# Layer A's residual addition on GpSimd beside attention, and the last closing statistics queued later

## The chip, the cores and the metric

The program runs on one core of a Trainium2 chip. The metric is the device time of one execution in microseconds. Three runs of the kernel before gave 1640.73, 1641.19 and 1642.21 us.

## What is computed

Four layers, A B A B, each added to its input x (2048 rows of 640 columns, 32 heads of 20):

```
x = x + A(layernorm(x)); x = x + B(layernorm(x)); and both once more

A: q, k, v = split(x @ wqkv)            # linear attention, phi(t) = t+1 or exp(t), + 1e-6
   out = phi(q) (phi(k)^T v) / (phi(q) . sum(phi(k)) + 1e-6) @ wo

B: in 4 segments of 512 rows, per head:
   a_dot = softmax(q k^T * scale + mask) v          # within the segment
   a_mem = phi(q) M / (phi(q) z + 1e-6)             # M, z: memory of the earlier segments
   out = (g * a_mem + (1 - g) * a_dot) @ wo;  M += phi(k)^T v;  z += sum(phi(k))
```

The mask leaves, for key k and query q of a segment, what lies on one side of the diagonal. g is a sigmoid of beta.

## The kernel before

**Tiling.** The rows are cut in 4 segments of 4 tiles of 128 rows. Products are done with fp16 operands in an upper and a lower part (three matmuls for one), so nearly every evacuation of a bank has a ScalarE copy of the upper part and a VectorE subtraction for the lower. There are 8 PSUM banks (`bank`) and a pool of 11 row buffers, tag `row`, which hold x, its residual input `xo`, its new value `xn`, the normed `xh`, the transposed outputs `oT` and layer A's queries `pqi`.

**Layer A.** A first pass over all segments (`g_first`) makes one matrix of keys and rows and writes the queries' features to DRAM (`pqd`). Then `merge` folds the matrix with the weights of v and o into one weight `wm`. The second pass makes the outputs segment by segment: `a_head` and `p_read` load the queries of a tile (line 924, on SyncE's queue), multiply them by z (line 934), sum them per head (938), add and scale (939), take the reciprocal (940) and multiply by it on GpSimd (942); this is the reading. `turn` transposes the result. `a_second` then multiplies by `wm` in two halves of 320 columns, 15 matmuls each, and `o_half` scales each half and adds the residual: by one VectorE instruction (line 499), or, with `later`, by a ScalarE copy (496) and a GpSimd addition (497). It then stores the tile (line 988, a DMA issue on ScalarE's queue) and takes its mean and variance (`moments`, 368 to 373: statistics and aggregate on VectorE, a power on GpSimd), shifts the mean (378), norms the tile (`normed`, 404) and transposes it for layer B.

**Layer B.** `b_project` makes v, q and k of a segment from the transposed tiles; q and k are split (`split_store`, 1020 to 1035) and go through DRAM. `attention` works in groups of 4 heads, eight groups a segment, each in three stretches: scores, row maxima (1224), their split in two parts (1233, 1234), a transposition and a small ScalarE copy that brings them back as two rows (1242 to 1247), scores the other way round, exponentials (1263), a GpSimd select that cuts them at the diagonal (1270), the weighing by v (1286), and the division. `read_mem` adds the memory's part. `b_out` multiplies by wo and adds the residual; it is what is called closing rows in the text below. It always uses the later path, except at the very end, and stores on ScalarE's queue (1185) behind an instruction named `anchor`. In the first layer B it also takes the statistics of each new tile (`gather`, 386 and 387), one tile late, behind the lower part of the next transposition, and after the last tile `settle` makes the inverse deviations of all four (393 on VectorE, 394 on GpSimd). They are used when the rows are loaded again for the next layer A.

**What runs beside what.** `run` merges two streams, the dense layers and attention, by estimated costs of TensorE. The four segments of layer A's second pass are followed by the projection of the same segment in layer B; from the end of segment 0's projection on, attention of the earlier segments runs between them. The closing rows of segments 0 and 1 are woven into the projections of segments 2 and 3, and `a_head` of the next segment follows directly behind them in the projection of segment 2.

**What sets the order.** TensorE's instructions run in the order in which the program names them. On the other engines Tile's planner queues them at build time by priority, which is the order of naming, among those that its own model of time holds ready; `tc.high_priority(offset=n)` moves a block n places ahead, or behind where n is negative, and `tc.issue_after(i)` puts a block behind instruction i on i's engine. On the chip each engine works its queue off in that order, waits included. `a_second` uses `self.added`, the last VectorE addition of `o_half`, as such a fence: for the shift of the mean and for the lower parts of two transpositions. Its `moments` go 40 places behind.

Of the kernel before, what the change touches and what calls it, by code (L numbers as in the profile page):

```python
# [25 lines left out]
NT = SEG // P  # L26
# [118 lines left out]
class Kernel:  # L145
# [816 lines left out]
    def a_second(self, src, dst, s, L, box, norm):  # L962


        nc = self.nc
        o, oT = box["o"], box["oT"]
        xT = self.x_t() if norm else None
        xh = []
        for i in range(NT):
            if i + 3 < NT:  # L970
                yield from self.p_read(L, s, i + 3, o)
            x = self.load_x(src, s, i, "xo")
            xn = self.row("xn")
            t = iter(())
            if i + 1 < NT:
                oT.append(self.new_oT())
                t = self.turn(o[i + 1], oT[i + 1], 0)
            for n in range(2):
                yield from (c for c in [next(t, None)] if c)
                self.o_half(oT[i], L["wm"], "G", x, xn, n)  # L980
                if norm and i > 0 and n == 0:
                    with self.tc.issue_after(self.added.ins):
                        m = self.shift(*m)
                    if i != 2:
                        xh.append(self.normed(*m))
                yield self.COST_N
            r = s * SEG + i * P
            self.q_x.dma_start(dst[r:r + P], xn)
            if norm:
                if i > 1:  # L990
                    yield from self.turn(xh[i - 2], xT, i - 2, self.added)
                if i == 2:
                    with self.tc.issue_after(self.upper.ins):
                        xh.append(self.normed(*m))
                with self.tc.high_priority(offset=-40):
                    m = self.moments(xn, False)
        box["xT"] = xT

        def tail():
            t = self.turn(xh[NT - 2], xT, NT - 2)  # L1000
            yield next(t)
            cost = next(t)
            with self.tc.issue_after(self.lower.ins), self.tc.issue_after(self.spread.ins):
                xh.append(self.normed(*self.shift(*m)))
            yield cost
            yield from self.turn(xh[NT - 1], xT, NT - 1)
        box["tail"] = tail()
# [141 lines left out]
    def b_out(self, st, wo, src, dst, norm, after=None):  # L1149

        yield lambda: st.get("attended")
        nc, s = self.nc, st["s"]
        made = []
        mv = self.sb.tile([P, NT, 2], F32, tag="mv4", name="mv4", bufs=NSEG) if norm else None
        begun = [None, None]
        turned = lambda i: self.o_turned(st, i)
        t = iter(()) if "oT" in st else turned(0)
        oT = st["oT"]
        if st.get("ends"):
            ahead = turned(1)  # L1160
            yield from (c for c in [next(t, None)] if c)
            yield next(ahead)
            for n in range(2):
                begun[n] = self.proj_n(oT[0], wo, 0, n, cs=range(3))
                yield 9 * HN * COL
        yield from t
        for i in range(NT):
            x = self.load_x(src, s, i, "xo")
            xn = self.row("xn")
            if i + 1 < NT:  # L1170
                t = ahead if i == 0 and st.get("ends") else turned(i + 1)
            else:
                t = self.o_turned(after, 0) if after and after.get("attended") else iter(())
            for n in range(2):
                yield from (c for c in [next(t, None)] if c)
                self.o_half(oT[i], wo, "B", x, xn, n, later=not st.get("ends"), begun=begun[n] if i == 0 else None)
                split = st.get("ends") and i == NT - 1
                if split:
                    c = slice(n * HN, (n + 1) * HN)
                    self.q_x.dma_start(dst[s * SEG + i * P:s * SEG + i * P + P, c], xn[:, c])  # L1180
                yield self.COST_N
            r = s * SEG + i * P
            if not split:
                with nullcontext() if st.get("ends") else self.tc.issue_after(self.anchor.ins):
                    self.q_x.dma_start(dst[r:r + P], xn)
            made.append(xn)
            if norm and i > 0:
                with self.tc.issue_after(self.lower.ins):
                    self.gather(made[i - 1], mv[:, i - 1])
        if norm:  # L1190
            yield 0.0
            self.gather(made[-1], mv[:, NT - 1])
            st["norm"] = self.settle(mv, False)


    def stacks(self, st, g):
# [367 lines left out]
```

## Time and profile before

| | us |
|---|---|
| median of three runs | 1641.19 |
| the profiled execution | 1644.86 |
| its span, first to last instruction | 1641.3 |
| TensorE busy | 1607.0 |
| VectorE busy | 1223.1 |
| ScalarE busy | 1016.0 |
| GpSimd busy | 518.2 |

PE is TensorE's matmuls, PEld its weight loads, DVE VectorE, ACT ScalarE, POOL GpSimd, SP SyncE; a q behind the name is the engine's queue. L499 is line 499 of the kernel. `xn<-ps,ioG,xo` says what an instruction writes and reads. The TensorE clock was granted in full for 0.999 of the span.

### The profile page before, as it was taken

What the parts mean: (1) busy time and instruction counts of PE and PEld (TensorE: products, weight loads), DVE (VectorE), ACT (ScalarE), POOL (GpSimd) and SP (SyncE); (2) the same over time, 40 slices, a digit from 0 to 9 for tenths busy, and PEclk for the clock granted to TensorE, in tenths of its full rate; (3) what the DMA queues carried; (4) which work ended last, traced back from release to release, by engine and by line L of the source; (5) the groups of instructions that cost most, each with busy time, mean ns of one, the idle gap of its engine ahead of it and who ended that gap; (6) DMA issues with size and microseconds to landing.
All of it is one profiled execution on the core that took longest, in us unless ns stands there. A gap on an engine that the chain in (4) does not pass through costs nothing.

```text
span 1641.3 us, 37783 instructions
## 1 busy us (share of the span) xinstructions
PE 1607.0 (98%) x13772; PEld 1016.2 (62%) x13772; DVE 1223.1 (75%) x3953; ACT 1016.0 (62%) x1955; POOL 518.2 (32%) x1077
## 2 busy tenths in 40 slices
PE   9999999999999999999999999999999999999998
PEld 6777776654665575456567777756546546645555
DVE  8777794688877787768764557837888888878772
ACT  6877743367567657667666544433775675676773
POOL 3421132133234423433341301211333433333552
PEclk9999999999999999999999999999999999999999
DMA  6434734423222422352211303534232232323432
GB/s 227 161 140 153 275 125 160 141 70 112 95 71 88 137 100 94 109 191 70 66 46 47 107 33 125 177 131 131 68 112 90 102 111 88 118 84 108 152 101 97
DMA packets 110345, 189.30 MB, mean 115 GB/s; under 512 B 14160, under 2 KB 69840, under 8 KB 107728
## 3 DMA queue, kind: packets, MB, share of 16 engines
q1 hardware_dynamic: 97536, 141.02, 26.6%
q0 software_dynamic: 3264, 24.91, 4.2%
q10 hardware_dynamic: 9360, 20.98, 3.3%
q8 instruction: 108, 1.77, 0.5%
q14 instruction: 77, 0.63, 0.1%
HBM read 109.32 MB, written 77.00 MB: 114 GB/s over the span
## 4 chain that ended last, share of the span: by engine, by line
PE 73%; ACT 5%; DVE 3%; issue 1%; DMA 1%; POOL 0%; SPq 0%; ACTq 0%; DVEq 0%
PE ps L431 29%; PE ps L417 14%; PE ps L1286 9%; PE ps L1259 4%; PE ps L348 4%; PE ps L758 4%; PE ps L1218 4%; ACT pe L1263 3%; PE ps L473 2%; PE ps L1299 1%; PE ps L1065 1%; DVE ps L1224 1%; PE ps L1055 1%; DMA pqi<-pqd 1%; ACT xh L404 0%
## 5 line engine op out<-in xcount | busy, mean ns | idle before, releaser
L1224 DVE CUSTOM_DVE_ANT_0 ps<-ps,maskw 128x384 f32<-128x384 f32 (+3 forms) x1024 | 472.4, 519 | 47.2 <-PE ps L1218 43.5
L1263 ACT ACTIVATE pe<-ps,lsc 128x512 f32<-128x512 f32 x640 | 391.7, 696 | 84.3 <-PE ps L1259 69.8
L1270 POOL TENSOR_SCALAR_AFFINE_SELECT pe<-pe 128x256 f32<-128x256 f32 (+1 forms) x640 | 238.7, 382 | 342.9 <-ACT pe L1263 338.2
L431 PEld LDWEIGHTS <-xT 128*128 128x128 f16 x2760 | 267.8, 98 | 103.6 <-issue 5.3
L431 PEld LDWEIGHTS <-oT 128*128 128x128 f16 x1920 | 185.8, 98 | 77.2 <-issue 4.6
L1286 PE MATMUL ps<-pe,v 128*32 128x512 f32 (+3 forms) x2048 | 156.5, 436 | 7.6 <-DVE nat L1026 3.2
L417 PE MATMUL ps<-xT,w_Bq 128*128 128x512 f16 x600 | 142.2, 382 | 3.6 <-ACT pe L1263 2.9
L1224 DVE DVE_READ_ACCUMULATOR2_ANT mg<- 128x1 f32 x1024 | 143.4, 140 | 0.0
L431 PE MATMUL ps<-w_Bo,oT 128*128 128x320 f16 x960 | 140.6, 299 | 1.9 <-DVE tmp L1309 0.6
L417 PE MATMUL ps<-xT,w_Bk 128*128 128x512 f16 x600 | 141.6, 379 | 0.4 <-DVE tmp L1309 0.4
L431 PE MATMUL ps<-wm,oT 128*128 128x320 f16 x960 | 140.6, 299 | 0.5
L431 PE MATMUL ps<-w_Bv,xT 128*128 128x320 f16 x960 | 139.7, 299 | 0.3 <-ACT pe L1263 0.3
L758 PE MATMUL ps<-pk,xs 128*128 128x321 f16 (+1 forms) x960 | 137.0, 300 | 1.5 <-DVE v L778 0.6
L431 PE MATMUL ps<-w_Aq,xT 128*128 128x320 f16 x960 | 138.4, 299 | 0.0
L1259 PE MATMUL ps<-qs,ks 62*128 62x512 f16 (+3 forms) x1024 | 130.2, 299 | 3.5 <-ACT pe L1263 2.4
L1026 DVE SCALAR_TENSOR_TENSOR nat<-ps,nat 128x512 f16<-128x512 f32 x80 | 55.2, 690 | 94.0 <-ACT r L1025 70.6
L431 PE MATMUL ps<-w_Ak,xT 128*128 128x320 f16 x840 | 119.4, 299 | 0.0
L758 PEld LDWEIGHTS <-xs 128*128 128x128 f16 x960 | 93.0, 97 | 39.6 <-issue 2.7
L1218 PE MATMUL ps<-ks,qs 60*128 60x512 f16 (+3 forms) x1024 | 115.2, 297 | 2.2 <-ACT pe L1263 1.9
L446 DVE SCALAR_TENSOR_TENSOR e<-e,r 128x320 f32<-128x320 f32 x120 | 60.4, 503 | 69.9 <-ACT r L445 69.4
L1286 PEld LDWEIGHTS ps<-pe,v 128*32 128x32 f32 x2048 | 63.0, 109 | 65.6 <-issue 45.3
L352 ACT ACTIVATE oT<-ps 128x384 f16<-128x384 f32 (+1 forms) x128 | 56.2, 445 | 72.8 <-PE ps L348 59.4
(236 smaller groups left out, 2396.1 us busy)
## 6 DMA issues: line engine op xcount, KB each, us to landing
x<-xn ACTq DMA_DIRECT2D x48, 320.0 KB
qs<-qd SPq DMA_DIRECT2D x128, 120.0 KB
ks<-kd SPq DMA_DIRECT2D x128, 120.0 KB
xo<-x SPq DMA_DIRECT2D x48, 320.0 KB
pqi<-pqd SPq DMA_DIRECT2D x32, 320.0 KB
qd<-nat SPq DMA_DIRECT2D x40, 256.0 KB
kd<-nat SPq DMA_DIRECT2D x40, 256.0 KB
x<-in_A_x SPq DMA_DIRECT2D x16, 320.0 KB
```

The costliest lines, as they stand in the source:

```text
L348: nc.tensor.transpose(pt[:, (c - c0) * P:(c - c0 + 1) * P], src[:, c * P:(c + 1) * P], self.ident)
L352: self.upper = nc.scalar.activation(hi, v, AF.Copy)
L417: nc.tensor.matmul(p, w[:, c, a, t * P:(t + 1) * P], xT[:, c, b, :], start=k == 0, stop=k == 3 * C - 1)
L431: nc.tensor.matmul(p, xT[:, c, a, i * P:(i + 1) * P], w[:, c, b, n * HN:(n + 1) * HN], start=k == 0, stop=k == 3 * C - 1)
L446: nc.vector.scalar_tensor_tensor(e, e, 1.0, r, op0=OP.min, op1=OP.add)
L758: nc.tensor.matmul(p, xs[:, i, a, c * P:(c + 1) * P], pk[i][:, b, cols], start=i == 0 and a == b, stop=i == NT - 1 and a == 1)
L1218: nc.tensor.matmul(bs[par][:, a:a + n], qs[r, p, i * P:(i + 1) * P], ks[r, p, :n], start=True, stop=True)
L1224: nc.vector.tensor_tensor_reduce(bs[par][:, a:a + n], bs[par][:, a:a + n], self.maskw[:, SEG - n:], 1.0, NEG, OP.add, OP.max, G["mg"][:, p ...
L1259: nc.tensor.matmul(b[:, a:a + n], ks[r, p, j * P:(j + 1) * P], qs[r, p, j * P:], start=True, stop=True)
L1263: nc.scalar.activation(e, b, AF.Exp, scale=self.lsc)
L1270: self.select = nc.gpsimd.affine_select(d, d, pattern=pat, compare_op=OP.is_ge, fill=0.0, base=0, channel_multiplier=-1)
L1286: nc.tensor.matmul(G["pv"][32 * h4:32 * h4 + 32, j * P:], v[j][:, h * E1:h * E1 + 32], G.pop((p, par, j)), start=j == 0, stop=j == 2, skip ...
```

## The change

In `a_second`, the tiles of segments 1 to 3 take the later path of `o_half` (`norm` is true in both layers A). The later path doesn't set `self.added`. In `b_out`, the statistics of the last tile and `settle` of segments 0 and 1 get a priority 100 places behind their own. Only the first layer B has `norm`.

```diff
@@ -977,7 +977,7 @@
             for n in range(2):
                 yield from (c for c in [next(t, None)] if c)
-                self.o_half(oT[i], L["wm"], "G", x, xn, n)
+                self.o_half(oT[i], L["wm"], "G", x, xn, n, later=s > 0 and norm)
                 if norm and i > 0 and n == 0:
                     with self.tc.issue_after(self.added.ins):
                         m = self.shift(*m)
@@ -1189,8 +1189,9 @@
         if norm:
             yield 0.0
-            self.gather(made[-1], mv[:, NT - 1])
-            st["norm"] = self.settle(mv, False)
+            with self.tc.high_priority(offset=-100) if s < 2 else nullcontext():
+                self.gather(made[-1], mv[:, NT - 1])
+                st["norm"] = self.settle(mv, False)
```

## Rows read from the trace of the kernel before

**Rows 1.** The page, part 1: busy us (share of the span) xinstructions.

```profile
PE 1607.0 (98%) x13772; PEld 1016.2 (62%) x13772; DVE 1223.1 (75%) x3953; ACT 1016.0 (62%) x1955; POOL 518.2 (32%) x1077
```

**Rows 2.** Busy time by stretch, the six of layer A beside attention, summed.

```profile
sum 177.00, PE 176.24 PEld 126.56 DVE 156.92 ACT 81.93 POOL 53.31; mean PE 29.37 PEld 21.09 DVE 26.15 ACT 13.65 POOL 8.88
```

**Rows 3.** TensorE's waits, whole span: us in total, times, longest us.

```profile
PE ps L1286 <- DVE nat L1026: 3.2, 5, 1.0
PE ps L417 <- ACT pe L1263: 2.9, 3, 1.9
...
PE ps L348 <- POOL pqi L942: 1.3, 1, 1.3
```

**Rows 4.** Groups by line: xcount | busy us, mean ns | idle before, releasers.

```profile
L497 POOL TENSOR_TENSOR xn<-xn,xo 128x320 f32<-128x320 f32 x56 | 49.8, 890 | 143.8 <-ACT xn L496 140.0 <-issue 2.9 <-POOL pe L1270 0.8
...
L499 DVE SCALAR_TENSOR_TENSOR xn<-ps,ioG,xo 128x320 f32<-128x320 f32 x64 | 34.7, 544 | 12.3 <-PE ps L431 11.2 <-DMA xo<-x 0.8 <-PE ps L348 0.3
...
L496 ACT ACTIVATE xn<-ps,ioB 128x320 f32<-128x320 f32 x56 | 29.7, 532 | 46.2 <-PE ps L431 42.2 <-DMA x<-xn 1.9 <-DVE st L386 1.3
```

**Rows 5.** Timeline, segment 2's end: start us, us, engine, line [idle before <-releaser].

```profile
463.49 0.93 ACT L404 ACTIVATE xh<-xn,nb,rs 128x640 f32<-128x640 f32 x1
...
467.89 0.55 PE L348 MATMUL ps<-ident,xh 128*128 128x128 f32 x3
...
467.78 0.43 DVE L1224 CUSTOM_DVE_ANT_0 ps<-ps,maskw 128x256 f32<-128x256 f32 x1 [1.49 <-PE ps L1218]
```

**Rows 6.** VectorE's waits, whole span: us in total, times, longest us.

```profile
DVE nb L378 <- POOL rs L373: 3.3, 6, 1.1
```

**Rows 7.** Timeline, 452 to 455 us, the four engines around one weighing.

```profile
452.04 0.55 DVE L499 SCALAR_TENSOR_TENSOR xn<-ps,ioG,xo 128x320 f32<-128x320 f32 x1 [0.96 <-PE ps L431]
...
452.42 1.27 ACT L1263 ACTIVATE pe<-ps,lsc 128x512 f32<-128x512 f32 x2 [1.63 <-PE ps L1259]
...
453.75 0.41 POOL L1270 TENSOR_SCALAR_AFFINE_SELECT pe<-pe 128x256 f32<-128x256 f32 x1 [0.16 <-ACT pe L1263]
...
454.34 0.75 PE L1286 MATMUL ps<-pe,v 128*32 128x128 f32 x12
```

**Rows 8.** Timeline of ScalarE in the closing rows of segment 0.

```profile
513.99 0.27 ACT L1244 ACTIVATE mt<-pm 32x128 f16<-32x128 f16 x1 [1.41 <-PE ps L1218]
```

**Rows 9.** Line 386 from 500 to 560 us, 8 readings: idle before them, times.

```profile
  POOL xn L497: 4.3, 2
```

**Rows 10.** Timeline, 546 to 563 us: VectorE, TensorE and SyncE's queue.

```profile
550.20 0.18 DVE L1234 SCALAR_TENSOR_TENSOR m<-mg,m 128x16 f16<-128x16 f32 x1
553.93 0.49 DVE L386 BATCH_NORM_STATS2 st<-xn 128x6 f32<-128x320 f32 x1 [3.56 <-POOL xn L497]
...
557.56 0.49 DVE L386 BATCH_NORM_STATS2 st<-xn 128x6 f32<-128x320 f32 x1 [0.75 <-POOL xn L497]
...
562.66 0.55 PE L348 MATMUL ps<-ident,pqi 128*128 128x128 f32 x3 [1.31 <-POOL pqi L942]
...
546.42 0.82 SPq L924 DMA_DIRECT2D pqi<-pqd  x2
```

**Rows 11.** Timeline of GpSimd and VectorE in the closing rows of segment 1.

```profile
702.21 0.86 POOL L497 TENSOR_TENSOR xn<-xn,xo 128x320 f32<-128x320 f32 x1
...
702.30 0.80 DVE L1234 SCALAR_TENSOR_TENSOR m<-mg,m 128x16 f16<-128x16 f32 x1
```

**Rows 12.** The chain of waits, 552 to 563 us: start us, us, what.

```profile
557.56 0.49 DVE st L386
...
558.77 0.12 DVE mv L387
...
559.57 0.08 DVE rs L393
...
559.75 1.05 POOL rs L394
...
560.80 1.81 POOL pqi L942
```

## Prediction

> **What bounds the kernel now.** I read the page's busy shares first: TensorE is busy for 98% of the span and no other engine comes near [rows 1]. So an edit is worth only the time by which it shortens or lengthens a wait of TensorE. The second view is the table by stretch. I cut out the six stretches in which layer A's output tiles are made beside attention (segments 1 to 3, twice): 312 to 336, 435 to 466, 584 to 616 us, and again from 1125, 1247 and 1381 us. Together they last 177.0 us; TensorE is busy for 176.24 of that, VectorE for 156.9 (89%), ScalarE for 81.9 (46%), GpSimd for 53.3 (30%) [rows 2]. VectorE is crowded there, but TensorE hardly waits: 0.76 us in all six. The third view, TensorE's waits over the whole span, says where it does wait: mostly for ScalarE's exponentials and VectorE's split of q and k in the projections, and once, for 1.3 us, for a product on GpSimd [rows 3]. That one wait is what the second edit is about.
>
> **Part 1: the output tiles.** It removes 48 instructions of VectorE (6 segments x 4 tiles x 2 halves) of 544 ns [rows 4]: 26.1 us, 4.4 us a segment. It adds 48 ScalarE copies, whose like takes 532 ns in the closing rows, 25.5 us, and 48 GpSimd additions of 890 ns, 42.7 us [rows 4]. In the six stretches that makes ScalarE 107 of 177 us busy, GpSimd 96, VectorE 131: none is full. So the result is set by waits, not by sums of busy time.
>
> What TensorE can win there is bounded by its idle time, 0 to 0.76 us. A backlog of VectorE doesn't reach past the stretches either: at 466 to 468 us VectorE stands idle for 1.49 us until TensorE gives it the next scores [rows 5]. I take half of the idle time, 0.4 us.
>
> What it can cost, place by place:
> - *The tile itself comes later*: 0.53 + 0.89 us instead of 0.54, with a hand-off some 1.0 us a half. The reader is the norm, then the transposes. In segment 2 the third tile's norm ends at 464.4 us and its first transpose starts at 467.89 [rows 5]: 3.5 us of cover. If the cover were gone, the price would be that 1.0 us a tile, at most three tiles a segment. I take 0.
> - *The fence*: the later path doesn't set `self.added`, so the shift of the mean and two transposes' lower parts, which were put behind a VectorE addition, stand behind an old one, that is, behind nothing. The shift may then follow its power on GpSimd directly and hold VectorE. Such holds are in the trace: 6, 3.3 us in total, longest 1.1 [rows 6]. 18 shifts at 0.55 us would be 9.9 us of VectorE, against 20.1 us idle and 26.1 us freed. I take 0 on TensorE.
> - *ScalarE's and GpSimd's queues ahead of a weighing*: there is one tight spot in each of the four stretches of segments 2 and 3. In segment 2 a projection ends at 452.0 us (VectorE's addition starts at 452.04), ScalarE starts the last two exponentials at 452.42, GpSimd's second select on them ends at 454.16, and TensorE's matmuls that follow start some 0.2 us later [rows 7]. A copy in front of the exponentials ends about 0.1 us into them; an addition that starts at 452.6 ends near 453.5, 0.3 us into the first select, and the second then ends 0.1 to 0.2 late. Cost: 0, if the addition is queued behind the selects, up to 0.53 + 0.89 - 0.2 = 1.2 us a spot if both go in full in front, 4.9 us in all. By the times of segment 2 I take 0.05 a spot, 0.2 us.
> - *The stores*: 24 DMA issues on ScalarE's own queue now wait for GpSimd instead of VectorE; exponentials, transposes' upper parts and attention's small copy are queued behind. The closing rows have the same order: there the queue stood 1.41 us before that small copy [rows 8], and no wait of TensorE over 0.15 us follows it. I take 0; a rival below has it otherwise.
> - *Statistics behind another engine*: VectorE's statistics now read what GpSimd writes. Among the closing rows of segment 0 only 2 of 8 readings were held for that, 4.3 us [rows 9], and both came after attention's split of its last row maxima there (553.93 and 557.56 us against 550.20, [rows 10]). Beside attention none of six was. I take 0.
>
> A rule that speaks against this part. The row first: at 702.21 us an addition like the new ones runs on GpSimd, and VectorE's split of the row maxima, begun at 702.30, takes 0.80 us and ends with it [rows 11], where the same instruction took 0.18 at 550.20 [rows 10]. The Trainium skill ("SBUF — State Buffer", section "Who interferes with whom") says that a VectorE instruction with two SBUF inputs contends with a GpSimd instruction that reads SBUF, and that whoever comes second waits in full; by that, the trace agrees. The sum above holds nothing for it, because the maxima are read late: a further rival prices it.
>
> **Part 2: the last statistics of the closing rows.** Four kinds of instruction go behind: two statistics, their aggregate, one addition (VectorE), one power (GpSimd), for segments 0 and 1 of the first layer B; no DMA moves with them. In segment 0 the reading that follows is layer A's next one (the queries loaded, scaled, normalized and multiplied on GpSimd). The chain of waits from 556 to 563 us runs through exactly these: statistics at 557.56, the power from 559.75 to 560.79, and only then the product, 560.80 to 562.61 [rows 12]. TensorE stood 1.31 us for it [rows 10]. Before that VectorE was held at the two statistics for 3.56 and 0.75 us, with the reading queued behind; its queries had been issued for loading at 546.42 [rows 10], seven microseconds before the first hold ended. Without the statistics in front, what releases the product moves ahead by at least 0.75 (the second hold), 0.49 (the statistics), 0.12 and 0.08 (the rest of them on VectorE's part of the chain): 1.4 us; and the power is out of GpSimd's way. The product then starts by 559.4 and, even at its long 1.81 us, ends by 561.2; TensorE came at 561.35. So the whole 1.31 us goes. Bounds: 0 (if the queue's order hardly moves) to 1.3 us; I take 1.3. Next late would be the second tile's product, 1.2 us after the first, which TensorE takes up only when the next stretch begins.
>
> In segment 1 no such reading follows and TensorE doesn't wait for what is moved: 0. The statistics themselves are wanted only when the rows are loaded again for the next layer, over 100 us later for segment 0. The tile that they read is kept some microseconds longer, one of eleven buffers: 0.
>
> **Sum**: -0.4 + 0.2 - 1.3 = -1.5 us. The profiled execution took 1644.86 us (span 1641.3), 3.7 above the median of the runs; from 1644.86 the sum gives 1643.4, and from the median, 1641.19, it gives **1639.7**.
>
> **The rivals.**
> - *Freed VectorE time pays later* (faster). TensorE's five waits for the split of q and k, 3.2 us [rows 3], lie in the projections just after the six stretches. If a less crowded VectorE started earlier on them and on the other banks it frees, 2.4 us might go besides the 1.5: 1637.3. For: VectorE is the most used engine after TensorE. Against: the idle 1.49 us at the end of a stretch [rows 5].
> - *The store holds ScalarE* (slower). The issue waits in ScalarE's queue for GpSimd's addition, about 1.0 us each; where an exponential stands behind that TensorE wants, TensorE pays. If 6 of the 24 stores did so: +6.0, so 1645.7. It decides from five stores on, the number that outweighs 1.5 and 0.2%. For: the hold of 1.41 us [rows 8] and TensorE's 2.9 us for the exponentials [rows 3]. Against: that hold cost TensorE nothing seen.
> - *The reading doesn't move up*: the planner leaves the order of 553 to 561 us nearly as it is, part 2 brings 0: 1641.0.
> - *The shared inputs of VectorE and GpSimd*: one split of the maxima a stretch is met by an addition and loses 0.80 - 0.18 = 0.62 us, six times, all of it on TensorE: 3.7 - 1.5 = +2.2, 1643.4. Against: in segment 2 it came 6 us before its use. By the Trainium skill's rule above ("SBUF — State Buffer", section "Who interferes with whom") the loss is there wherever the two meet.
>
> **How the numbers follow.** Chances: forecast 0.55, VectorE's freed time 0.22, the stores 0.12, the reading not moved 0.08, the shared inputs 0.03. A measurement of this kernel can tell about 0.2%, 3.3 us, from no change. Faster by more: 0.25 (the first rival and the forecast's lower edge), slower by more: 0.12, within: 0.63. The forecast's own range is 1638.4 to 1641.2. The range for 8 in 10 is 1636.2 to 1644.4: it takes in the first rival but for its far part (0.07) and leaves out the stores' far part (0.11); the select's upper bound, 4.9 - 1.7 = +3.2, is its top.
>
> **What would show it.** Right: no wait of TensorE for GpSimd's product near 562 us, the reading on VectorE before the last statistics; VectorE's busy time down by about 26 us, GpSimd's up by 43; TensorE's idle time in the six stretches still around 1 us. Wrong: new waits of TensorE for exponentials or selects in those stretches, ScalarE idle before a store there, statistics held on the additions beside attention, or the waits in the projections changed by more than a microsecond.

## The result and the profile after

The changed kernel took 1646.34 us (median of 7 runs, 1644.97 to 1647.98), the kernel before, timed beside it, 1641.17 (7 runs). The ratio is 1.0027, with an interval from 1.0017 to 1.0036: slower by 0.27%, 5 us, where 1639.7 was forecast, and above the top of the range, 1644.4.

The profiled execution of after took 1645.11 us, its span is 1643.2. The page's busy times, to be held against [rows 1], then two groups by line (their times: xcount | busy us, mean ns of one | idle time of the engine before them), to be held against [rows 4]:

```profile
PE 1609.9 (98%) x13772; PEld 1017.0 (62%) x13772; DVE 1202.7 (73%) x3905; ACT 1036.0 (63%) x2003; POOL 556.6 (34%) x1125
...
L497 POOL TENSOR_TENSOR xn<-xn,xo 128x320 f32<-128x320 f32 x104 | 91.3, 878 | 234.9 <-ACT xn L496 230.4 <-issue 2.9 <-POOL pe L1271 0.8
...
L368 DVE BATCH_NORM_STATS2 st<-xn 128x6 f32<-128x320 f32 x64 | 31.0, 488 | 33.7 <-POOL xn L497 33.3
```

The work moved, by somewhat less than the arithmetic had it (26.1, 25.5 and 42.7 us): VectorE 20.4 us less, ScalarE 20.0 more, GpSimd 38.4 more. (Line numbers above 1190 are one higher in after.) The last row is the one to read: at line 368, the statistics of layer A's tiles, VectorE now stands idle for 33.3 us behind GpSimd's additions. In the trace of before it stands there for 0.7 us in all, never over 0.04 us at a time and never behind another engine. The table of VectorE's waits (us in total, times, longest) says the same, and that the holds of the shift, 3.3 us in 6 in before [rows 6], have become 14. The third row is of the trace of before, the closing rows' statistics over the whole of it:

```profile
DVE st L368 <- POOL xn L497: 33.3, 30, 2.4
...
DVE nb L378 <- POOL rs L373: 9.4, 14, 1.1
...
DVE st L386 <- POOL xn L497: 19.8, 10, 3.6
```

So VectorE was relieved of some 20 us of work and was held for 39 us more at lines 368 and 378, with everything that is queued behind them. One of the longest holds, in the timeline of VectorE, ScalarE, GpSimd and TensorE (start us, us, engine, line, [idle before <-releaser]):

```profile
449.97 0.48 DVE L483 TENSOR_TENSOR otok<-ps,rc 128x320 f32<-128x320 f32 x1
452.84 0.49 DVE L368 BATCH_NORM_STATS2 st<-xn 128x6 f32<-128x320 f32 x1 [2.39 <-POOL xn L497]
453.25 0.54 DVE L354 TENSOR_TENSOR oT<-ps,oT 128x384 f16<-128x384 f32 x1
...
450.71 0.53 ACT L496 ACTIVATE xn<-ps,ioG 128x320 f32<-128x320 f32 x1 [1.11 <-PE ps L431]
451.14 0.48 ACT L352 ACTIVATE oT<-ps 128x384 f16<-128x384 f32 x1
...
452.84 0.33 ACTq L988 DMA_DIRECT2D x<-xn  x1
...
451.22 0.77 POOL L1271 TENSOR_SCALAR_AFFINE_SELECT pe<-pe 128x256 f32<-128x256 f32 x2
451.95 0.86 POOL L497 TENSOR_TENSOR xn<-xn,xo 128x320 f32<-128x320 f32 x1
...
454.18 0.55 POOL L373 TENSOR_TENSOR rs<-rs,mhalf 128x1 f32<-128x1 f32 x1 [1.37 <-DVE rs L372]
454.70 0.87 POOL L497 TENSOR_TENSOR xn<-xn,xo 128x320 f32<-128x320 f32 x1
455.53 0.76 POOL L1271 TENSOR_SCALAR_AFFINE_SELECT pe<-pe 128x256 f32<-128x256 f32 x2
...
455.06 1.91 PE L1287 MATMUL ps<-pe,v 128*32 128x384 f32 x24
```

And the same 24 matmuls in before:

```profile
453.58 1.51 PE L1286 MATMUL ps<-pe,v 128*32 128x384 f32 x24
```

ScalarE's copy ends at 451.24, GpSimd's addition waits behind two selects and ends at 452.81, and VectorE, which had nothing left to do at 450.4 but had the reading at the head of its queue, stands until 452.84. The split of line 354 behind it could have run from about 451.6, when ScalarE's upper part was there. The store's issue in ScalarE's queue is released at the same moment. From there the hold goes on through GpSimd's queue: the variance comes late, so GpSimd's power (line 373) waits 1.37 us for it and ends at 454.73, the next addition stands behind the power, and attention's two selects stand behind the addition. The 24 matmuls of the weighing, which read what the selects write, take 1.91 us in place of 1.51, and the trace calls none of that idle.

As idle time of TensorE the loss is seen only in segment 1, best around 330 and 336 us, here with TensorE's rows:

```profile
328.29 0.15 DVE L372 TENSOR_SCALAR rs<-mv 128x1 f32<-128x1 f32 x1
329.11 0.21 DVE L378 TENSOR_SCALAR nb<-mv,rs 128x1 f32<-128x1 f32 x1 [0.67 <-POOL rs L373]
...
328.53 0.55 POOL L373 TENSOR_TENSOR rs<-rs,mhalf 128x1 f32<-128x1 f32 x1 [1.70 <-DVE rs L372]
...
330.04 2.20 PE L431 MATMUL ps<-wm,oT 128*128 128x320 f16 x15 [0.53 <-DVE mg L1225]
...
335.47 0.49 DVE L368 BATCH_NORM_STATS2 st<-xn 128x6 f32<-128x320 f32 x1 [0.74 <-POOL xn L497]
...
335.47 0.33 ACTq L988 DMA_DIRECT2D x<-xn  x1
335.84 0.44 ACT L451 ACTIVATE v<-ps 128x320 f32<-128x320 f32 x1 [2.38 <-PE ps L1260]
...
334.57 0.86 POOL L497 TENSOR_TENSOR xn<-xn,xo 128x320 f32<-128x320 f32 x1
...
336.33 1.38 PE L431 MATMUL ps<-w_Bv,xT 128*128 128x320 f16 x9 [0.28 <-ACT v L451]
```

At 329 us the shift, whose fence is gone, holds VectorE for GpSimd's power, the row maxima behind it come late, and TensorE waits 0.53 us for a bank. At 335 us statistics and store are held together, ScalarE's copy of v stands behind the store, and TensorE waits 0.28 us for that copy. In segments 2 and 3, which bear 3.8 of the 6.0 us measured below, TensorE has 0.13 us of idle time in each of the four stretches, 0.12 in before: there the loss is in rows that take longer, as the weighing above does.

Two more measures stand beside the medians below. TensorE's 13772 matmuls have the same order in all these kernels, so they can be matched one by one: the **growth of the six stretches** is how much longer the work of 312 to 345, 435 to 470, 584 to 620, 1125 to 1158, 1247 to 1284 and 1381 to 1418 us (times of before) took than in the first trace of before. The second trace of before differs from the first by 0.0 in each of them, and the three traces with the changed tiles as they are (the first of after, e0, e2) give 6.0, 5.9 and 5.8, so tenths count. The other is the span: in some executions of every kernel TensorE runs a few us at half its clock near 1350 us, which makes the span 1 to 2 us longer, so **spans** are medians over executions whose mean granted clock was 1.0 (n of them). Some 1.9 us of a time lie outside the span.

| kernel | median us (runs) | ratio [interval] | span (n) | six stretches |
|---|---|---|---|---|
| before (three timings) | 1641.72, 1641.76, 1642.24 (24, 27, 27) | 1 | 1639.3, 1639.4, 1639.1 (16, 18, 14) | 0.00 |
| e0 changed again | 1646.10 (7) | 1.0025 [1.0015, 1.0036] | 1642.8 (3) | +5.88 |
| e1 part 2 alone | 1641.37 (11) | 0.9997 [0.9988, 1.0006] | 1637.9 (6) | 0.00 |
| e2 part 1 alone | 1646.54 (7) | 1.0031 [1.0020, 1.0042] | 1644.2 (4) | +5.78 |
| e3 VectorE adds | 1638.37 (10) | 0.9978 [0.9969, 0.9987] | 1635.1 (6) | -1.53 |
| e4 e3, no fence | 1640.95 (11) | 0.9993 [0.9984, 1.0002] | 1638.5 (7) | +0.73 |
| e5 store unheld | 1648.37 (5) | 1.0038 [1.0025, 1.0051] | 1645.7 (2) | +7.53 |
| e6 statistics unheld | 1640.40 (11) | 0.9992 [0.9983, 1.0000] | 1638.2 (8) | +0.77 |
| e7 both unheld | 1640.12 (11) | 0.9991 [0.9982, 1.0000] | 1638.1 (6) | +0.07 |
| e8 e3 without part 2 | 1638.67 (11) | 0.9981 [0.9972, 0.9990] | 1636.5 (8) | -1.52 |
| e9 statistics behind a split | 1642.67 (11) | 1.0005 [0.9996, 1.0014] | 1640.2 (7) | +3.06 |
| e10 first halves alone | 1640.22 (11) | 0.9993 [0.9984, 1.0002] | 1638.2 (9) | +1.37 |

### The profile page after: what moved, and what is told of

Same layout as the page of the kernel before. It is cut to its first block, busy times and chain, and to the rows that moved or that the text cites. A ratio compares the mean times of both kernels' runs of the same rounds, so it can differ in the third digit from the quotient of the medians.

```text
span 1643.2 us, 37843 instructions
## 1 busy us (share of the span) xinstructions
PE 1609.9 (98%) x13772; PEld 1017.0 (62%) x13772; DVE 1202.7 (73%) x3905; ACT 1036.0 (63%) x2003; POOL 556.6 (34%) x1125
## 4 chain that ended last, share of the span: by engine, by line
PE 73%; ACT 5%; DVE 2%; issue 2%; POOL 1%; DMA 0%; ACTq 0%; SPq 0%; DVEq 0%; POOLq 0%
PE ps L431 29%; PE ps L417 14%; PE ps L1287 9%; PE ps L1260 5%; PE ps L758 4%; PE ps L348 4%; PE ps L1219 4%; ACT pe L1264 3%; PE ps L473 2%; PE ps L1300 1%; PE ps L1055 1%; PE ps L1065 1%; DVE ps L1225 1%; ACT xh L404 1%; POOL xn L497 0%
## 5 line engine op out<-in xcount | busy, mean ns | idle before, releaser
L497 POOL TENSOR_TENSOR xn<-xn,xo 128x320 f32<-128x320 f32 x104 | 91.3, 878 | 234.9 <-ACT xn L496 230.4
```

Of the source, the lines that this page charges most:

```text
L497: nc.gpsimd.tensor_tensor(xn[:, c], xn[:, c], x[:, c], op=OP.add)
```

## The experiments

**Which part, and which engine.** Four kernels: the changed one again (e0), each part alone, and both parts with ScalarE's scaling kept but the residual added on VectorE, which is then the fence again.

> The changed kernel again, as the mark for the others. By the two traces matched matmul by matmul, the changed one loses some 1.2 us in each of the two stretches of segment 1 and 0.7 to 1.0 us in each of the four of segments 2 and 3, and gains 1.4 us at the reading near 562 us: +3.5 us where neither execution has a clock dip. If that ledger is complete, the median stands 3 to 5 us over the kernel before; if there is more that no trace shows, 5 us or more.

Part 2 alone (e1) is the diff without its first hunk, part 1 alone (e2) without its second.

> Only the last statistics of the closing rows go behind; layer A's tiles as before. If the two edits are independent, TensorE's wait of 1.31 us for the product near 562 us is gone and nothing else moves: -1.3 to -1.4 us, 1639.8. If the gain needs the new tiles beside it, or is given back in segment 3, the time is that of before within 0.5 us.

> Only layer A's tiles change. Independent edits: +4.9 to +6.5 us, that is 1.4 us over the full change, with the wait near 562 us back. If the late statistics themselves cost something (their buffers, the queue), it is as fast as the full change or faster.

```diff
 # e3: the changed kernel, and in o_half
-            nc.gpsimd.tensor_tensor(xn[:, c], xn[:, c], x[:, c], op=OP.add)
+            add = (nc.vector if own else nc.gpsimd).tensor_tensor(xn[:, c], xn[:, c], x[:, c], op=OP.add)
+            if own:
+                self.added = add
 # and in a_second: o_half(..., later=s > 0 and norm, own=True)
```

> Both edits, but VectorE adds the residual behind ScalarE's copy, and its addition is the fence again; GpSimd gets nothing new, ScalarE's 48 copies stay. Theory GpSimd (the additions come late and hold VectorE's statistics and shifts, the stores on ScalarE's queue, and the selects): all of that is gone, -1 to 0 us against before, 1640.2 to 1641.2, some 5 us better than the full change. Theory ScalarE (the 48 copies in front of exponentials and transposes cost the time): no better than the full change, +4 to +6 us. Theory crowded VectorE: it now has 25 us more than in the full change, so it would be about 0 to +1 us against before.

The loss repeats (e0, 1.0025), all of it is part 1's (e2, 1.0031), and it isn't ScalarE's share in it: with the same copies and VectorE adding (48 additions of 491 ns in place of 544) the kernel is faster than before, 0.9978. So the price is that of putting GpSimd between ScalarE and VectorE, the lost fence with it: 1635.1 to 1643 us in span, 7.4 us in the six stretches (-1.53 to +5.88). By spans part 2 brings 1.4 us (1639.3 to 1637.9), though its median does not tell it from nothing.

At its place, the trace of e1 from 554 to 562 us, VectorE, GpSimd and TensorE:

```profile
554.14 0.49 DVE L386 BATCH_NORM_STATS2 st<-xn 128x6 f32<-128x320 f32 x1 [3.57 <-POOL xn L497]
...
558.39 0.18 DVE L939 TENSOR_SCALAR rca<-rca 128x32 f32<-128x32 f32 x1
559.56 0.83 DVE L934 TENSOR_TENSOR pqi<-pqi,z 128x640 f32<-128x640 f32 x1 [1.00 <-DMA pqi<-pqd]
560.30 0.35 DVE L940 RECIPROCAL rca<-rca 128x32 f32<-128x32 f32 x1
...
560.73 1.27 POOL L942 TENSOR_TENSOR pqi<-pqi,rca 128x640 f32<-128x640 f32 x1 [2.99 <-DVE rca L940]
...
562.05 0.55 PE L348 MATMUL ps<-ident,pqi 128*128 128x128 f32 x3 [0.50 <-POOL pqi L942]
```

And one row of VectorE from the trace of before:

```profile
560.66 0.81 DVE L934 TENSOR_TENSOR pqi<-pqi,z 128x640 f32<-128x640 f32 x1
```

The second hold is gone from in front of the reading, as forecast. But the product starts at 560.73, as good as when it did before, 560.80 [rows 12]: the place of the statistics was taken by the multiplication of the third tile, which waits 1.00 us for its queries to be loaded, with the first tile's reciprocal (ready at 558.6) queued behind it. TensorE's wait shrinks from 1.31 us [rows 10] to 0.50 because the product takes 1.27 us in place of 1.81 and TensorE comes 0.2 later. The 1.81 goes with what VectorE does beside it: in before the multiplication by z of another tile (the row above) runs at the start of the product, in e1 only sums (line 938). In all the traces the 64 products with that multiplication beside them for over half a microsecond take 1.70 to 1.81 us, the 384 others 1.26 to 1.32, but for 14 of 1.54. In after the wait is gone (1.35 us won), because there the third tile's queries keep VectorE waiting for only 0.40 us. It hangs on that load: in e4, e6 and e10 it is there in time and TensorE doesn't wait; in e0, e3, e7 and e9 VectorE waits for it 0.87 to 1.11 us, and TensorE 0.37 to 0.61. So part 2 brings 0.7 to 1.5 us at its place.

**The fence.** From e3, the one line is taken out that makes VectorE's addition the fence.

```diff
             add = (nc.vector if own else nc.gpsimd).tensor_tensor(xn[:, c], xn[:, c], x[:, c], op=OP.add)
-            if own:
-                self.added = add
```

> The kernel that keeps ScalarE's scaling but lets VectorE add the residual (1638.4 us), with one thing taken from it: its additions no longer set self.added, so the shift of the mean and the transposes' lower parts lose their place behind them, as in the changed kernel. If the lost fence is what costs (shifts that hold VectorE for GpSimd's power, 0.66 to 0.75 us each in the changed kernel's trace): 3 to 5 us of the 8 come back, 1641 to 1643. If the fence costs nothing by itself and the cost lies in who waits for GpSimd's additions: within 1 us of 1638.4.

The fence costs by itself: 1638.37 to 1640.95 us, 1635.1 to 1638.5 in span, 2.3 us in the stretches. The rows of e3 (lines two higher), VectorE and TensorE:

```profile
328.23 0.16 DVE L372 TENSOR_SCALAR rs<-mv 128x1 f32<-128x1 f32 x1
328.41 0.70 DVE L1227 CUSTOM_DVE_ANT_0 ps<-ps,maskw 128x512 f32<-128x512 f32 x1
...
330.59 0.21 DVE L378 TENSOR_SCALAR nb<-mv,rs 128x1 f32<-128x1 f32 x1
...
329.58 1.67 PE L431 MATMUL ps<-wm,oT 128*128 128x320 f16 x11
```

And of e4:

```profile
328.25 0.15 DVE L372 TENSOR_SCALAR rs<-mv 128x1 f32<-128x1 f32 x1
329.13 0.21 DVE L378 TENSOR_SCALAR nb<-mv,rs 128x1 f32<-128x1 f32 x1 [0.73 <-POOL rs L373]
329.26 0.69 DVE L1225 CUSTOM_DVE_ANT_0 ps<-ps,maskw 128x512 f32<-128x512 f32 x1
...
330.06 1.11 PE L431 MATMUL ps<-wm,oT 128*128 128x320 f16 x7 [0.52 <-DVE mg L1225]
```

With the fence the maxima run first and the shift finds its power done; without it the shift stands 0.73 us, the maxima start 0.85 later, and TensorE waits 0.52. This price is that of the fence where VectorE adds; its share in the changed kernel was not measured by itself.

**Who waits for the addition.** In the next three GpSimd keeps all its 48 additions, but its sum goes into the residual's tile, and ScalarE's scaled copy stays in `xn`. The store, the statistics, or both then take the copy, which waits for nothing on GpSimd; the norm always reads the sum. What takes the copy leaves out the residual, so these three compute something else (e5 and e7 write tiles without it, e6 and e7 norm by statistics without it), and only their times are of use. That the sum goes into another tile is not what helps: e5 has that too.

```diff
-            nc.gpsimd.tensor_tensor(xn[:, c], xn[:, c], x[:, c], op=OP.add)
+            into = x if split else xn
+            nc.gpsimd.tensor_tensor(into[:, c], xn[:, c], x[:, c], op=OP.add)
 # e5: store xn, statistics of x;  e6: store x, statistics of xn;  e7: store and statistics of xn
```

> The changed kernel, but GpSimd's sum goes into the residual's tile, and the store to DRAM sends ScalarE's scaled copy without the residual: the store in ScalarE's queue then waits for nothing on GpSimd (the output lacks the residual of these tiles). Statistics and norm still read the sum. If the stores cost what TensorE lost: the wait for ScalarE's v copy (0.43 us at 335 us, twice in the run) and the late small copies go, 1643 or less. If the stores are only where the waits can be seen for two copies: -0.9 us, 1645.4. If ScalarE's order is not in it at all: 1646.2.

> The changed kernel, but VectorE's statistics of these tiles read ScalarE's scaled copy without the residual, so that they wait for nothing on GpSimd (the norm is taken with these statistics; the output differs). GpSimd's additions, the stores and the norm's reading of the sum stay. If the statistics that hold VectorE for GpSimd (0.5 to 2.4 us each in the changed kernel's trace) are the cost: most of the 5 us comes back, 1641 to 1643. If the additions in GpSimd's queue ahead of the selects, or the stores, are: 1645 to 1646.5.

> Both of the two edits before at once: neither the store nor the statistics wait for GpSimd's sum; GpSimd still makes all 48 additions and only the norm reads them. If the holds behind the additions are the cost, this stands where the kernel with VectorE's addition stands, 1638 to 1640. If GpSimd's work itself (in front of selects, against VectorE at the memory) is: 1644 to 1646.

The statistics decide. With them unheld (e6) the six stretches fall from +5.9 to +0.8 and the span from 1643 to 1638.2; the store still waits for GpSimd, the fence is still lost, the additions are all there. VectorE's waits in e6:

```profile
DVE st L368 <- ACT xn L496: 20.6, 30, 1.1
DVE nb L378 <- POOL rs L373: 10.4, 19, 1.1
```

Line 368 is still held 30 times, now for ScalarE's copy, but 0.69 us at a time and not 1.1: the reading is queued too early in either case, and GpSimd's part of the wait is what reaches TensorE. Freeing the store as well (e7) brings 0.7 us more in the stretches, all in segment 1, and nothing in the span. Freeing the store alone (e5) makes it worse, 1648.37, which none of the three expectations had. Segment 1 in e5, ScalarE, VectorE and TensorE:

```profile
334.20 0.44 ACT L451 ACTIVATE v<-ps 128x320 f32<-128x320 f32 x1 [1.24 <-PE ps L431]
...
334.80 0.49 DVE L368 BATCH_NORM_STATS2 st<-xo 128x6 f32<-128x320 f32 x1 [1.06 <-POOL xo L498]
...
335.64 0.41 DVE L354 TENSOR_TENSOR xT<-ps,xT 128x256 f16<-128x256 f32 x1
...
336.11 0.55 PE L348 MATMUL ps<-ident,xh 128*128 128x128 f32 x3 [1.19 <-DVE xT L354]
```

The copy of v no longer waits for the store, as the theory of the stores has it. But another order came with it: the held statistics now stand in front of a split that TensorE wants, and 0.28 us are traded for 1.19. In segments 2 and 3 TensorE's wait at line 473 grows to 0.85 us, once in each of the four stretches.

The matching also says where each kernel loses. Against e3, whose own gain of 1.5 us all of them share, the growth stands at six places, three in segment 1 (two stretches) and three in segments 2 and 3 (four stretches); us for each time, places by the times of after:

| kernel | 330 | 336 | 339 | 447 | 456 | 469 |
|---|---|---|---|---|---|---|
| after (e0, e2 alike) | 0.6 | 0.4 | 0.4 | 0.4 | 0.4 | 0.4 |
| e4 no fence | 0.6 | 0 | 0 | 0.3 | 0 | 0 |
| e5 store unheld | 0.3 | 1.3 | 0 | 1.1 | 0.4 | 0 |
| e6 statistics unheld | 0 | 0.1 | 0.4 | 0.4 | 0 | 0 |
| e7 both unheld | 0 | 0 | 0 | 0.4 | 0 | 0 |
| e9 statistics behind a split | 0 | 0.8 | 0 | 0 | 0.4 | 0.4 |
| e10 first halves alone | 0.7 | 0 | 0 | 0.4 | 0 | 0 |

So the holds of the statistics (e6) are behind four places: the maxima at 330, the copy of v at 336, the weighing at 456 by way of GpSimd's power, addition and selects, and at 469 four score matmuls that take 0.70 us in place of 0.38. This last one goes with the store's hold too (e5), and how it comes about was not found. At 339 it is the store (e7). What is left in e7 is 0.4 us at 447: by the rows ScalarE's norm now stands in front of the exponentials that TensorE's line 473 waits for (norm at 446.11, exponentials from 446.92 in after; exponentials from 444.41, norm at 445.55 in e3). So e7's +0.1 does not say that the additions cost nothing: it is 1.6 us above e3. That the norm's place is the cause was read, not tested. (In e4 the 0.3 at 447 is at line 431, behind a hold of the shift.) At 330 the wait goes with the fence kept (e3, e9) as well as with the statistics unheld and the fence lost (e6, e7).

**Part 1 without GpSimd, and repairs.** e8 is e3 without part 2. e9 is the changed kernel with the reading queued elsewhere. In e10 only the first half of a tile goes the new way (`later=s > 0 and norm and n == 0`).

> Part 1 alone with VectorE adding the residual: ScalarE scales the 48 half tiles, VectorE adds and stays the fence, the last statistics are where they were before. It parts the gain of the kernel that had both (1638.4 us). If the gain is the scaling on ScalarE (a bank of TensorE freed early): 1639 to 1639.5, faster than before by 2 to 2.5 us. If it is part 2's moved statistics: 1641 to 1641.7, the same as before.

```diff
 # e9, in a_second; late = s > 0 and norm
+                if late and i > 0 and n == 0:
+                    with self.tc.issue_after(self.lower.ins):
+                        m = self.moments(before, False)
                 self.o_half(oT[i], L["wm"], "G", x, xn, n, later=late)
-                if norm and i > 0 and n == 0:
-                    with self.tc.issue_after(self.added.ins):
+                if norm and i > 0 and n == late:
+                    with self.tc.issue_after((self.lower if late else self.added).ins):
                         m = self.shift(*m)
 ...
+                if late and i + 1 < NT:
+                    before = xn
+                else:
                     with self.tc.high_priority(offset=-40):
                         m = self.moments(xn, False)
```

> The changed kernel with nothing left out but another order on VectorE: the statistics of a tile are queued behind the next tile's first split (the lower part of its transposed rows) instead of in front of it, and the shift one half tile later. GpSimd still adds all 48 halves. If the statistics that hold VectorE are the cost, and the place in the queue cures it: 1641 to 1642.5. If they only come to be held at another place, or the norms come too late: 1645 to 1648.

> The changed kernel, but only the first half of each tile goes the new way (ScalarE, GpSimd); the second half is VectorE's one instruction as before, and is the fence again. The second half's addition is the one that the last reading of a tile waits for. If the holds and the lost fence are the cost, nearly all of it goes: 1640.5 to 1642. If each addition on GpSimd costs alike, half of it stays: 1643 to 1644.

e8 is faster than before, 0.9981 [0.9972, 0.9990]: the gain of e3 is that of scaling on ScalarE, 1.5 us in the stretches and 2.7 in span, and part 2 adds 1.4 (1636.5 to 1635.1). e3 has both and beats both kernels of the comparison; by medians it and e8 can't be told apart (1638.37 and 1638.67).

e9 brings 2.8 us of the 5.9 back by order alone, 1642.67, just over the 1641 to 1642.5 expected. Its holds on VectorE:

```profile
DVE st L368 <- POOL xn L497: 10.8, 13, 1.4
DVE nb L378 <- POOL rs L373: 5.3, 8, 1.1
```

Two thirds of the 33.3 us are gone, while VectorE's waits for ScalarE's copies in front of its splits grew by 12.3 us. What is left of its +3.1 is a new wait of TensorE for the copy of v (0.7 us, twice) and the losses at 456 and 469. e10 comes to 1640.22, as fast as before with half the additions on GpSimd (+1.4 in the stretches): its second half is VectorE's, so the last reading waits for nobody else (6.2 us of holds in 12 are left).

**The kernel before again.**

> The kernel before once more, for a second trace of it. In the first trace TensorE ran 3.4 us at half its clock around 1345 us, which by its length cost 1.7 us. If that belongs to that one execution, this span is 1639.3 to 1639.8 at a clock of 1.0; if it belongs to the kernel, the same dip stands at the same place.

The same half clock stands at the same place, span 1640.8. It isn't one execution's accident: it is in both traces of before, in e0, e2, e3, e5 and e8, and not in the other profiled executions; of the 78 timed executions of before about four in ten (30) have the clock of 0.999 that goes with it.

## Why the prediction was wrong

- **What bounds the kernel** was right, but the bound drawn from it was not. TensorE's idle time in the six stretches, 0.76 us [rows 2], was taken as the most that part 1 could win. e8 wins 1.5 there. Busy time hides short waits: 24 matmuls of the weighing took 1.91 us in place of 1.51 with no idle time between, and where the six stretches grew by 6.0 us, TensorE's idle time in them grew only from 1.3 to 3.2. What a table of busy time shows as idle is no ceiling for a gain, and no alarm for a loss.
- **The statistics behind GpSimd**, taken as 0 on TensorE, is the step that failed: 5.1 us (e6 against e0). I went by one segment's closing rows, where 2 of 8 readings were held [rows 9] and VectorE had done its urgent work first [rows 10], and by none of six being held beside attention. Over the whole trace of before, 10 of the 32 readings of the closing rows were held, 19.8 us. The changed tiles are queued less well still: 30 holds on 48 new readings, with splits and maxima behind them that TensorE wants, and GpSimd's power and selects behind those.
- **The lost fence** was seen with its mechanism and nearly its size (0.66 to 0.75 us a hold where 0.55 was put), but its 0 on TensorE was wrong: 2.3 us where VectorE adds (e4 against e3). In the changed kernel its share can't be told apart, since the wait at 330 us that it makes in e4 is gone in e6 and e7, which lack the fence too. The argument set the held time against VectorE's idle and freed time. It isn't a sum: a hold counts where it stands, in front of the maxima.
- **The stores**: 0 was near once the statistics are unheld, 0.7 us in all (e6 against e7), in segment 1. With the statistics held, the store's hold is in the places at 336 and 469 us too, but freeing it alone made the kernel slower (e5). The rival that was to end on the slower side, six stores at 1 us, gave 1645.7, near the measured time by luck: what held ScalarE briefly held VectorE for longer.
- **Selects ahead of a weighing** were mis-sized: 0.05 us a spot was taken, 0.4 is lost at each of the four spots (456 us), 1.6 in all and within the bound of 1.2 a spot. It needs the held statistics: in e6 and e7 it is 0.
- **The tile itself coming later** was taken as 0. What is found, 0.4 us at 447 us in four stretches, is not the norm's lateness but its place in ScalarE's queue.
- **Shared inputs**: no loss was traced to the additions meeting VectorE, although the single pair of rows [rows 11] is as the Trainium skill ("SBUF — State Buffer", section "Who interferes with whom") has it. A price that fits it does reach TensorE at part 2's place, where TensorE waited for the product of 1.81 us beside VectorE's multiplication.
- **Part 2** was right in size, in part by luck: forecast -1.3; at its place -0.8 alone, -1.35 in after and -0.9 in e0, by spans -1.4. Its path was half right: the reading did move up, but in e1 the product didn't, since the third tile's load took the place of the statistics (the wait 1.00 us above), and what was won there came from the product being shorter. The prediction looked at when the first two queries were loaded, not the third. Where the third is loaded in time (e4, e6, e10), the product starts at 559.33 to 559.49, near the 559.4 forecast.
- **Freed VectorE time paying later**: not seen. e3 and e8, which leave VectorE as busy as before (1224.4 and 1221.6 us against 1223.1), win most, and no kernel that relieves it (e5, e6, e7, e9, e10) does as well.

The differences of neighbours in the chain e3, e4, e7, e6, e0 (+2.3, -0.7, +0.7, +5.1) end at the measured +5.9 by construction, so that is no proof of the single terms, and the table of places shows that e4's loss is not part of e7's. Beside the stretches there are part 2 and -0.32 us at 1524 us (which e5 and e7 don't win; they lose 0.6 and 0.4 there): in all +4.3 for the first trace of after and +4.7 for e0, where the spans give +3.5 to +3.9. The two traces of before differ by 0.4 us outside the stretches; the rest is open.

## What to carry to other kernels

When work is moved to another engine, list the readers of its result and what is queued behind each of them: one relieved engine that must now wait for the helper can lose more than it was spared, and the cost is at the place of the hold, not in sums of busy or idle time. A step that leaves its engine takes its fences along, so give what was queued behind it a new one. Here, handing the first operation to the free engine and keeping the last one on the engine of the readers (scaling on ScalarE, addition on VectorE) had the gain without the holds.

## What the runs showed of the hardware that was not expected

TensorE's clock falls for some 3 us near 1350 us in some executions and not in others, with the same matmuls and a pause of the same length before it. Busy time by stretch, of the second trace of before and then of after, two rows each (the stretch, its us, busy of PE, PEld, DVE, ACT, POOL, then the granted clock, the DMA's share and GB/s):

```profile
1345.00:1350.00 5.00, 3.06 (x26) 1.92 (x27) 3.29 (x14) 5.00 (x10) 4.38 (x8) 1.00 0.30 80
1350.00:1355.00 5.00, 4.62 (x21) 1.80 (x19) 4.10 (x12) 2.67 (x6) 1.67 (x4) 0.66 0.42 157
```

```profile
1350.00:1355.00 5.00, 3.06 (x25) 1.64 (x24) 3.41 (x11) 4.92 (x10) 4.16 (x7) 1.00 0.56 173
1355.00:1360.00 5.00, 4.51 (x82) 2.48 (x81) 4.72 (x16) 2.59 (x5) 1.21 (x3) 1.00 0.46 140
```

In both TensorE is busy for 3.06 us of 5; then the mean granted clock is 0.66 in the one (part of the stretch at the lower level, 1.2 GHz) and 1.00 in the other. It makes spans 1 to 2 us longer, as much as the effects that were looked for, and it is no property of either kernel: the spans of either come in both kinds. The 0.999 of the profiled execution of before is such a mean over its span, with one short stretch at 1.2 GHz, and not the share of the span at the full clock.
